# The transfers of an attention loop on SyncE put in the order of the source, and a weight chunk moved within a pair of heads

## The chip, the cores and the metric

The kernel runs on one core of one Trainium2 chip. The metric is the device time of one execution in microseconds (us). Before the change three runs took 875.57, 877.01 and 880.34, median 877.01.

A core has TensorE (PE, with its weight loads shown apart as PEld), VectorE (DVE), ScalarE (ACT), GpSimd (POOL) and SyncE (SP). SP computes nothing here; it issues transfers (DMAs). ACT issues some of its own, between its computations.

## The reference

Attention of 4 batches x 8 heads over 768 positions with heads of 64, in which a query sees only the keys whose 6-bit hash is its own, and then a feed-forward block with w_in (512 x 2048) and w_out (2048 x 512):

```python
q_bits = (np.einsum('bhsd,dk->bhsk', q, proj) > 0).astype(np.int64)
k_bits = (np.einsum('bhsd,dk->bhsk', k, proj) > 0).astype(np.int64)
...
mask = q_bucket[:, :, :, None] == k_bucket[:, :, None, :]
scores = scale * np.matmul(q, k.transpose(0, 1, 3, 2))
scores = np.where(mask, scores, -1000000000.0)
...
attn = attn / (np.sum(attn, axis=-1, keepdims=True) + 1e-09)
return np.matmul(attn, v).astype(np.float32)
...
h = x @ w_in
g = h * (1.0 / (1.0 + np.exp(-1.702 * h)))
return (g @ w_out).astype(np.float32)
```

The weights reach the core as 64-bit floats and are converted there.

## The kernel before

The attention works on 16 pairs of heads, n = 0 to 15; `attention` (L289) runs them in a software pipeline, and the loop over n = 1 to 15 (L625) holds in one turn work of several pairs. A pair has two halves of its queries, c = 0 and 1, and six tiles of 128 keys. Its scores come in groups (c, first key tile) of two key tiles each: (0,0), (0,2), then the values of the pair before (L524, `values`), then (0,4), (1,0), the values of this pair's half 0, then (1,2), (1,4). From pair 3 on (`BY_PARTS`) `scores_of_four` (L477) makes a group by three passes of 32-row matmuls at L491: over the hash features (`feat`), over `own` (q and k of the pair, transposed) and over `other` (the same rows with the 32-row halves of each head exchanged; the profile shows it as `s_in`, whose room it uses, and so it does for `own` of every third pair). All six groups take their PSUM places in turn from four. Each tile of scores goes through an exponential on ACT (L463). `unload` (L532, L535 and L536) takes finished values from PSUM to `xT` on ACT, which frees that place for a group of scores.

What a turn n of the loop prepares for later pairs:

- The hash of pair n+1: `featured(n + 1)` thresholds it on DVE (L446), and eight transfers of 12 KB carry it to `feats` (L454, `feat<-f`). `spread(n + 1)` copies these rows again by two transfers (L459, `feat<-feat`), which read what the eight wrote, and calls `exchange(n + 1)`, four transfers of 192 KB from `own` to `other` (L424, `s_in<-own` or `s_in<-s_in`).
- `fetch(n + 3, "k")` and `fetch(n + 3, "q")` load the raw k and q by four transfers each (L353), once `turn(n + 2)` (a DVE transpose, L417) and `measure(n + 2)` (an ACT pass over the same tile that bounds its size, L431) have read the tile's last contents. `fetch_v(n + 1)` loads v by two transfers (L365).
- A chunk of w_in, 512 KB, is loaded and converted. `begin(n)` (L576) starts it with a transfer on ACT (L165); its next steps are DVE operations (L181, L185, L189, L196, L200, L203) and one of ACT (L193), called by `step` at fixed places of the turn. There is one tile `raw` for it, so that a chunk's transfer follows the last step (L203) of the chunk before. In the turn of before, `begin(n)` stands behind the exponentials of (0,0) and (0,2).

The order on PE, DVE, ACT and POOL is the order of the source (`ORDERED`, L18). The order on SP is not: a scheduler places SP's transfers by its own estimate of when each could start. A queue runs strictly in its order; a transfer that waits holds up all behind it on that engine, and on ACT the computations too. Transfers of SP and ACT take eight completion semaphores in turn, in the order in which the scheduler placed them, and one takes a semaphore over only when the transfer that had it eight places earlier has landed.

As built, SP's row of 24 transfers in a turn from pair 6 on is: 8 features, 2 spreadings, 4 k, 2 v, 2 exchanges, 4 q, 2 exchanges, where the exchanges are those of pair n+2, one turn ahead of where the source has them. In turns 4 and 5 some exchanges stand among the features and spreadings, in turns 2 and 3 spreading and exchanges come behind k and v.

After the attention comes the feed-forward (`feed_forward`, L816), 539 us of the span.

Of the kernel before, what the change touches and what calls it, by code (L numbers as in the profile page):

```python
# [19 lines left out]
P = 128  # L20
# [18 lines left out]
def kernel(  # L39
# [17 lines left out]
    nc = tc.nc  # L57

    loader = [nc.sync]
    B, H, S, D = q.shape  # L60
# [7 lines left out]
    HS = HT * P  # L68
# [41 lines left out]
    for i, x in enumerate("kq"):  # L110
# [7 lines left out]
        for c in range(2):  # L118
            r0 = D * i + 32 * c
# [41 lines left out]
    def convert(cv, dst, src, queue=None, psum=None):  # L161


        raw = cv.tile([P, CW, 2], U32, tag="raw", name="raw")
        (queue or loader[0]).dma_start(out=raw, in_=src)  # L165
# [11 lines left out]
        yield  # L177


        if psum is None:  # L180
            nc.vector.scalar_tensor_tensor(part, hi, 3, masks[0x3FFFFFFF], op0=Alu.logical_shift_left, op1=Alu.bitwise_and)  # L181
# [107 lines left out]
    def attention(ff):  # L289
# [4 lines left out]
        with actx:  # L294
# [39 lines left out]
                nc.gpsimd.memset(*x)  # L334

            raws, vts, xts = {}, {}, {}

            def behind(x):

# [2 lines left out]
            def fetch(n, name):  # L342

                b, hp = pairs[n]
                x = raws[n, name] = ld.tile([P, S // 32, 32], F32, tag=name, name=name)
                if (n, name) == (2, "q"):
                    behind(x[:, 0, 0:1])
                src = {"k": k, "q": q}[name]
                for j in range(2):
                    rows = src[b, 2 * hp + j].rearrange("(s p) (a i) -> a p s i", p=32, i=32)  # L350
                    for a in range(D // 32):
                        r0 = D * j + 32 * a
                        loader[0].dma_start(out=x[r0 : r0 + 32], in_=rows[a])  # L353

            def fetch_v(n):
                b, hp = pairs[n]
                x = ld.tile([P, T, 2, D], F32, tag="v", name="v", bufs=2)
                if n == 0:
                    x = x.rearrange("p t j d -> p (t j d)").rearrange("p (j t d) -> p t j d", j=2, d=D)
                vts[n] = x  # L360
                if n == 1:
                    behind(x[:, 0, :, 0])
                for j in range(2):
                    order = "(t p) d -> p t d" if n else "(p t) d -> p t d"
                    loader[0].dma_start(out=x[:, :, j, :], in_=v[b, 2 * hp + j].rearrange(order, p=P))  # L365

            def first_pair():

# [50 lines left out]
            def exchange(n):  # L419

                for j in range(2):
                    for i in range(2):
                        r0, r1 = D * j + 32 * i, D * j + 32 * (1 - i)
                        loader[0].dma_start(out=other[n % 3][r0 : r0 + 32], in_=own[n % 3][r1 : r1 + 32])  # L424

            def measure(n, name):

# [16 lines left out]
            def featured(n):  # L444
                f = wk.tile([P, HS], BF16, tag="f", name="f", bufs=2)
                nc.vector.tensor_scalar(f, dots.pop(n), above[:, 0:1], weight[:, 0:1], op0=Alu.is_gt, op1=Alu.mult)  # L446
                yield
                for c in range(2):
                    for i, x in enumerate("kq"):

                        queue = nc.scalar if (n, x, c) == (1, "q", 0) else nc.sync
                        for j in range(2):
                            r0 = D * i + 32 * c + 16 * j
                            queue.dma_start(out=feats[n % 2][x][D * j : D * j + 16, c * HS : (c + 1) * HS], in_=f[r0 : r0 + 16, :])  # L454

            def spread(n):

                for j in range(2):
                    loader[0].dma_start(out=both[n % 2][D * j + 32 : D * j + 48], in_=both[n % 2][D * j : D * j + 16])  # L459
                exchange(n)  # L460

            def weigh(n, c, kt, ps):
# [14 lines left out]
            def scores_of_four(n, groups):  # L477

                for c, k0 in groups:
                    if n < BY_PARTS:  # L480
                        scores(n, c, (k0, k0 + 1))
                        continue
                    cols = slice(c * HS, (c + 1) * HS)
                    ps = [in_turn() for _ in range(2)]
                    f, x, y = feats[n % 2], own[n % 3], other[n % 3]
                    for at, (a, m) in enumerate(((f["k"], f["q"]), (x[:, 0], x[:, 1]), (y[:, 0], y[:, 1]))):
                        for i in range(2):
                            keys = slice((k0 + i) * P, (k0 + i + 1) * P)
                            for j in range(2):
                                r0 = D * j + 32 * i  # L490
                                nc.tensor.matmul(ps[i][:, j, 0:HS], a[r0 : r0 + 32, keys], m[r0 : r0 + 32, cols],  # L491
                                                 start=at == 0, stop=at == 2)
                    for i in range(2):
                        weigh(n, c, k0 + i, ps[i])
# [926 lines left out]
    def whole(steps):  # L1421
        for _ in steps:
            pass
# [49 lines left out]
```

## Time and profile before

| | |
|---|---|
| median of three runs | 877.01 us (875.57 to 880.34) |
| the profiled execution | 875.73 us, its span 873.9 us |
| PE busy | 851.7 us (97%) |
| DVE busy | 692.5 us (79%) |
| ACT busy | 335.9 us (38%) |
| POOL busy | 367.8 us (42%) |
| transfers issued by SP (queue q1) | 111.42 MB, 48.0% of 16 DMA engines' span |
| transfers issued by ACT (queue q10) | 31.62 MB, 10.8% |
| attention | up to 334.6 us |

How to read it: a row of a timeline is start, length (us), engine, line, operation, tile written <- tiles read, number of instructions, and in brackets the idle time before it with what ended it. "SPq" and "ACTq" are the issuing of a transfer, not its run. A row of the waits is engine, line <- what was waited for, then us in total, times, longest. What ended a wait is inferred from semaphores: a wait in front of a transfer that ACT issues is shown at the next computation of ACT.

### The profile page before, as it was taken

How to read it: one execution, taken by the hardware profiler on the slowest of the kernel's cores; microseconds unless marked ns; L12 is line 12 of the kernel's file. 1: busy time of each engine (PE TensorE's matmuls, PEld its weight loads, DVE VectorE, ACT ScalarE, POOL GpSimd, SP SyncE). 2: the span in 40 equal slices, each digit the busy share in tenths (PEclk: the TensorE clock that was granted, in tenths of full speed). 3: DMA queues.
4: the chain of work that ended last, by engine and by line, in shares of the span. 5: the costliest groups of instructions: out<-in, count | busy, mean ns of one | idle time of the engine just before them, and what ended most of it. 6: DMA issues, size and time to landing. Idle time of an engine off the chain costs nothing.

```text
span 873.9 us, 14972 instructions
## 1 busy us (share of the span) xinstructions
PE 851.7 (97%) x5631; PEld 524.7 (60%) x5631; DVE 692.5 (79%) x1069; ACT 335.9 (38%) x549; POOL 367.8 (42%) x321
## 2 busy tenths in 40 slices
PE   9999999999899999999999999999999999999996
PEld 4444444434344444465666666644888888888885
DVE  4478889888868997588788878766997977897786
ACT  5665656655566654344444444343100000000000
POOL 4333333433333437899773357678755100000000
PEclk9999999999999999999999999999999999999999
DMA  5768687777677401535455555568755575477534
GB/s 107 98 111 161 125 147 139 138 132 126 125 144 131 111 26 51 165 122 216 193 204 206 216 193 216 205 227 281 255 188 192 176 223 210 163 228 222 195 126 98
DMA packets 165197, 144.04 MB, mean 165 GB/s; under 512 B 124384, under 2 KB 139872, under 8 KB 159872
## 3 DMA queue, kind: packets, MB, share of 16 engines
q1 hardware_dynamic: 154704, 111.42, 48.0%
q10 hardware_dynamic: 10416, 31.62, 10.8%
q8 instruction: 45, 0.74, 0.4%
q14 instruction: 32, 0.26, 0.1%
HBM read 79.69 MB, written 50.33 MB: 149 GB/s over the span
## 4 chain that ended last, share of the span: by engine, by line
PE 67%; DVE 9%; DMA 8%; POOL 6%; SPq 4%; issue 3%; ACT 2%; ACTq 0%; DVEq 0%; POOLq 0%
PE product L1196 29%; PE product L869 16%; PE s L524 7%; PE small L937 5%; PE s L491 5%; DVE acc L515 3%; PE product L937 2%; PE s L474 2%; DMA feat<-f 2%; SPq L353 2%; DMA raw<-in_moe_w_in_dram 2%; SPq L454 1%; DMA q<-in_q_dram 1%; ACT e L463 1%; DMA k<-in_k_dram 1%
## 5 line engine op out<-in xcount | busy, mean ns | idle before, releaser
L463 ACT ACTIVATE e<-s 128x768 f32<-128x768 f32 x192 | 144.0, 812 | 51.1 <-PE s L491 41.9
L524 PE MATMUL s<-e,v 128*32 128x385 f32 x1536 | 131.9, 490 | 0.0
L502 POOL TENSOR_TENSOR t_x<-e 128x768 f32<-128x768 f32 x32 | 59.2, 1850 | 153.9 <-ACT e L463 139.3
L869 PE MATMUL product<-xT,w_in_sb 128*128 128x512 f32 x216 | 100.0, 593 | 0.1
L524 PEld LDWEIGHTS s<-e,v 128*32 128x32 f32 x1536 | 46.3, 109 | 81.1 <-issue 64.4
L869 PE MATMUL product<-t_x,s_in 128*128 128x512 f32 x192 | 89.5, 593 | 0.8 <-ACT u L991 0.8
L491 PE MATMUL s<-s_in 32*128 32x384 f32 x816 | 85.6, 488 | 1.6 <-DMA s_in<-own 0.8
L502 POOL TENSOR_TENSOR t_x<-t_x,e 128x768 f32<-128x768 f32 x32 | 56.2, 1756 | 51.6 <-ACT e L463 50.3
L515 DVE TENSOR_TENSOR acc<-acc,e 128x768 f32<-128x768 f32 x63 | 73.6, 1169 | 2.3
L1232 ACT COPY u<-product 128x256 f32<-128x256 f32 x20 | 7.4, 372 | 158.1 <-PE product L1196 124.9
L869 PEld LDWEIGHTS product<-xT,w_in_sb 128*128 128x128 f32 x216 | 40.9, 190 | 35.8 <-issue 32.5
L491 PEld LDWEIGHTS s<-s_in 32*128 32x128 f32 x816 | 43.1, 186 | 23.0 <-DMA s_in<-own 2.5
L869 PEld LDWEIGHTS product<-t_x,s_in 128*128 128x128 f32 x192 | 36.4, 190 | 30.8 <-issue 27.3
L491 PE MATMUL s<-own 32*128 32x384 f32 x432 | 46.6, 487 | 0.0
L491 PE MATMUL s<-feat 32*128 32x384 bf16 x312 | 32.2, 327 | 10.8 <-ACT xT L536 10.0
L885 DVE TENSOR_TENSOR u<-product,u 128x256 f32<-128x256 f32 (+1 forms) x60 | 28.4, 485 | 15.6 <-PE product L937 12.8
L491 PEld LDWEIGHTS <-feat 32*128 32x128 bf16 x312 | 10.4, 91 | 49.1 <-issue 37.0
L1196 PE MATMUL product<-raw_g,xT 128*128 128x256 f32 x152 | 35.1, 379 | 0.0
L225 POOL TENSOR_TENSOR u<-v,u 128x1024 f32<-128x1024 f32 (+1 forms) x11 | 23.8, 2167 | 21.5 <-ACT v L882 14.1
L226 POOL TENSOR_TENSOR v<-c,v 128x1024 f32<-128x1024 f32 (+1 forms) x15 | 32.4, 2157 | 1.0
L885 DVE TENSOR_TENSOR v<-product,v 128x512 f32<-128x512 f32 x24 | 16.5, 688 | 19.8 <-PE product L869 19.8
L512 DVE SCALAR_TENSOR_TENSOR acc<-t_x,e 128x768 f32<-128x768 f32 x31 | 29.3, 946 | 3.2 <-ACT e L463 2.5
(298 smaller groups left out, 1809.5 us busy)
## 6 DMA issues: line engine op xcount, KB each, us to landing
raw_g<-g_dram SPq DMA_DIRECT2D x20, 1024.0 KB, 5.1
s_in<-g_dram SPq DMA_DIRECT2D x20, 1024.0 KB, 5.1
g_dram<-c ACTq DMA_DIRECT2D x18, 512.0 KB, 2.9
raw<-in_moe_w_out_dram ACTq DMA_DIRECT2D x16, 512.0 KB, 3.7
raw<-in_moe_w_in_dram ACTq DMA_DIRECT2D x15, 512.0 KB, 3.8
s_in<-own SPq DMA_DIRECT2D x36, 192.0 KB, 4.4
v<-in_v_dram SPq DMA_DIRECT2D x32, 192.0 KB, 3.8
k<-in_k_dram SPq DMA_DIRECT2D x60, 96.0 KB, 3.1
```

The lines of the kernel that those rows point to most:

```text
L225: return [lambda: eng.tensor_tensor(t1, b12, b11, op=Alu.subtract), lambda: eng.tensor_tensor(b12, b22, b12, op=Alu.subtract), lambda: eng ...
L226: lambda: eng.tensor_tensor(b12, b22, b12, op=Alu.subtract),
L463: nc.scalar.activation(es[c][:, kt, :, 0:HS], ps[:, :, 0:HS], Act.Exp, scale=1.0 / D**0.5)
L491: nc.tensor.matmul(ps[i][:, j, 0:HS], a[r0 : r0 + 32, keys], m[r0 : r0 + 32, cols], start=at == 0, stop=at == 2)
L502: nc.gpsimd.tensor_tensor(low_sum, low_sum if i else e[:, 0], e[:, i + 1], op=Alu.add)
L512: nc.vector.scalar_tensor_tensor(acc, terms[0], T * TINY, terms[1], op0=Alu.add, op1=Alu.add)
L515: nc.vector.tensor_tensor(acc, acc, terms[i + 1], op=Alu.add)
L524: nc.tensor.matmul(av[D * j + d : D * j + d + 32, :], vt[:, t, j, d : d + 32], es[c][:, t, j, :], start=(t == 0), stop=(t == T - 1))
L869: nc.tensor.matmul(ps, wq[LEFT[i]][:, kc, :], xq[RIGHT[i]][:, kc, :], start=(start and kc == 0), stop=(kc == K2 - 1), skip_group_check=not ...
L885: nc.vector.tensor_tensor(dst, x, y, op=Alu.add)
L937: nc.tensor.matmul(x, wq[LEFT[i]], xq[RIGHT[i]], start=start, stop=True, skip_group_check=True)
L1196: nc.tensor.matmul(ps, wq[LEFT[i]][:, c, :], gq[RIGHT[i]][:, c, :], start=(onto is None and c == 0), stop=(c == F4 - 1), skip_group_check= ...
```

## The change

The transfers that SP issues in the attention from turn 2 on are held in the order of the source (`tc.keep_in_program_order`), by a helper `load` that takes the place of `loader[0].dma_start` in `fetch`, `fetch_v`, `exchange`, `featured` and `spread`. `spread(n + 1)` moves up in the turn, from behind `fetch_v(n + 1)` to ahead of `fetch(n + 3, "k")`. `begin(n)` moves from behind both first groups of exponentials to between them, and two dependencies without a semaphore (`behind_issue`) place the chunk behind the first feature transfer and the second feature transfer behind the chunk, in the scheduler's order alone. Nothing is added to or taken from what is computed or moved.

```diff
+            turns_kept = [False]
+            def load(out, in_):
+                dma = nc.sync.dma_start(out=out, in_=in_)
+                if turns_kept[0]:
+                    tc.keep_in_program_order(dma)
+                return dma
+            def behind_issue(dma, other):
+                tc.add_manual_dep(dma.ins, other.ins.name,
+                                  mybir.DependencyInfo(mybir.DependencyClass.NoSync, mybir.DependencyReason.DATA), reason="row")
...
             def begin(n):
                 if 0 <= n - 2 < len(in_chunks) - LATE:
                     conv[n] = convert(cv, *in_chunks[n - 2], nc.scalar)
-                    step(n)
+                    return next(conv[n])
...
+                    turns_kept[0] = True
+                    scores_of_four(n, ((0, 0),))
                     if n < last:
+                        first = next(features)
+                        chunk = begin(n)
+                        if chunk is not None:
+                            behind_issue(chunk, first)
+                            behind_issue(next(features), chunk)
                         whole(features)
-                scores_of_four(n, ((0, 0), (0, 2)))
+                    else:
+                        begin(n)
+                    scores_of_four(n, ((0, 2),))
+                else:
+                    scores_of_four(n, ((0, 0), (0, 2)))
                 if n == 2:
                     measure(3, "q")
                     fetch(4, "q")
-                begin(n)
...
                     if more:
                         measure(n + 2, "k")
+                    if n < last and n + 1 >= BY_PARTS:
+                        spread(n + 1)
                     if n + 3 <= last:
                         fetch(n + 3, "k")
...
                 if n < last:
                     fetch_v(n + 1)
-                    if n + 1 >= BY_PARTS:
-                        spread(n + 1)
```

As built, PE, DVE and POOL have the same instructions in the same order as before. On ACT the chunk's transfer stands behind the second exponential of a turn in place of the fourth. SP's row is now, in every turn from 3 on: 8 features of pair n+1, 2 spreadings and 4 exchanges of pair n+1, 4 k, 2 v, 4 q; the chunk takes its semaphore between the first and the second feature.

More of the change, by code (lines that the diff above doesn't have):

```diff
@@ L164, in convert @@
         raw = cv.tile([P, CW, 2], U32, tag="raw", name="raw")
-        (queue or loader[0]).dma_start(out=raw, in_=src)
+        dma = (queue or loader[0]).dma_start(out=raw, in_=src)
         def of(x):
@@ L176, in convert @@
             size = psum.tile([P, CW], F32, tag="size", name="size")
-        yield
+        yield dma
         if psum is None:
@@ L352, in fetch @@
                         r0 = D * j + 32 * a
-                        loader[0].dma_start(out=x[r0 : r0 + 32], in_=rows[a])
+                        load(x[r0 : r0 + 32], rows[a])
             def fetch_v(n):
@@ L364, in fetch_v @@
                     order = "(t p) d -> p t d" if n else "(p t) d -> p t d"
-                    loader[0].dma_start(out=x[:, :, j, :], in_=v[b, 2 * hp + j].rearrange(order, p=P))
+                    load(x[:, :, j, :], v[b, 2 * hp + j].rearrange(order, p=P))
             def first_pair():
@@ L423, in exchange @@
                         r0, r1 = D * j + 32 * i, D * j + 32 * (1 - i)
-                        loader[0].dma_start(out=other[n % 3][r0 : r0 + 32], in_=own[n % 3][r1 : r1 + 32])
+                        load(other[n % 3][r0 : r0 + 32], own[n % 3][r1 : r1 + 32])
             def measure(n, name):
@@ L449, in featured @@
                     for i, x in enumerate("kq"):
-                        queue = nc.scalar if (n, x, c) == (1, "q", 0) else nc.sync
                         for j in range(2):
                             r0 = D * i + 32 * c + 16 * j
-                            queue.dma_start(out=feats[n % 2][x][D * j : D * j + 16, c * HS : (c + 1) * HS], in_=f[r0 : r0 + 16, :])
+                            to, of = feats[n % 2][x][D * j : D * j + 16, c * HS : (c + 1) * HS], f[r0 : r0 + 16, :]
+                            if (n, x, c) == (1, "q", 0):
+                                nc.scalar.dma_start(out=to, in_=of)
+                            else:
+                                yield load(to, of)
             def spread(n):
                 for j in range(2):
-                    loader[0].dma_start(out=both[n % 2][D * j + 32 : D * j + 48], in_=both[n % 2][D * j : D * j + 16])
+                    load(both[n % 2][D * j + 32 : D * j + 48], both[n % 2][D * j : D * j + 16])
                 exchange(n)
@@ L635, in attention @@
                         step(n - 1)
+                    turns_kept[0] = True
+                    scores_of_four(n, ((0, 0),))
                     if n < last:
-                        whole(features)
-                scores_of_four(n, ((0, 0), (0, 2)))
+                        first = next(features)
[3 more added lines that the diff above has]
+                            behind_issue(next(features), chunk)
+                        whole(features)
+                    else:
+                        begin(n)
+                    scores_of_four(n, ((0, 2),))
+                else:
+                    scores_of_four(n, ((0, 0), (0, 2)))
                 if n == 2:
```

## The prediction

> **What bounds the kernel now.** I read the busy shares first, then the attention stage in windows, then the waits, then the timeline of one pair.
>
> ```profile
> span 873.9 us, 14972 instructions
> ```
> ```profile
> 66.78:88.50 21.72, 20.89 (x237) 9.09 (x240) 18.28 (x25) 12.80 (x22) 6.51 (x5) 1.00 0.84 159
> 88.50:272.20 183.70, 173.69 (x2092) 76.84 (x2096) 154.75 (x207) 113.43 (x190) 66.40 (x36) 0.99 0.73 134
> 253.68:272.20 18.52, 18.52 (x237) 8.26 (x240) 16.50 (x23) 12.61 (x22) 6.96 (x4) 1.00 0.72 136
> 272.20:310.13 37.93, 36.88 (x458) 16.40 (x459) 35.22 (x45) 22.98 (x39) 13.84 (x9) 1.00 0.48 103
> 334.60:873.90 539.30, 531.84 (x2011) 381.58 (x2011) 424.63 (x699) 131.82 (x213) 245.21 (x199) 1.00 0.56 193
> ```
>
> The columns are the stretch, its length, the busy time of PE, PEld, DVE, ACT and POOL, the granted clock, the DMA share and GB/s. I cut at the ends of the matmuls of L546, one per pair. Pairs 4 to 12 are the second row, 183.70 / 9 = 20.41 us each. Pair 12 (third row) has no idle time of PE and takes 18.52. So PE alone would need 18.5 a pair; the nine pairs have 9 x 1.89 = 17.0 us over that, and pair 3 (first row) has 3.2. This 20.2 us and the 1.05 that PE is idle in pairs 13 and 14 (fourth row, 37.93 - 36.88) are all that the change can win. The last row, the feed-forward, holds nothing that the diff touches.
>
> ```profile
> PE s L491 <- ACT xT L536: 10.0, 9, 2.3
> PE s L491 <- DMA s_in<-own: 0.8, 1, 0.8
> PE s L491 <- DMA s_in<-s_in: 0.8, 1, 0.8
> ```
> ```profile
> ACT xT L431 <- DMA feat<-f: 32.2, 10, 4.8
> DVE w_in_sb L181 <- DMA raw<-in_moe_w_in_dram: 20.7, 10, 3.8
> ```
>
> PE waits for the unloading of a PSUM tile by ACT (L536), ACT waits for a transfer of features. The timeline of ACT and PE in pair 8 (start, us, what) tells why:
>
> ```profile
> 177.43 0.33 ACTq L165 DMA_DIRECT2D raw<-in_moe_w_in_dram  x1
> 177.88 0.84 ACT L431 ACTIVATE xT<-k 128x768 f32<-128x768 f32 x1 [4.17 <-DMA feat<-f]
> 178.90 0.58 ACT L536 ACTIVATE xT<-s,vs 128x384 f32<-128x384 f32 x1
> ```
> ```profile
> 177.51 0.33 PE L491 MATMUL s<-feat 32*128 32x384 bf16 x2
> 179.53 0.34 PE L491 MATMUL s<-feat 32*128 32x384 bf16 x2 [1.69 <-ACT xT L536]
> ```
>
> ACT does not wait in L431. It waits in front of L165, whose transfer of the chunk takes its turn on a semaphore that a feature transfer of the same pair holds. Behind it stand the measuring (L431) and the unloading (L536), for which PE waits 1.69 us. What makes the features late is SyncE's row:
>
> ```profile
> 160.96 1.19 SPq L459 DMA_DIRECT2D feat<-feat  x2
> 167.09 4.16 SPq L353 DMA_DIRECT2D q<-in_q_dram  x4
> 171.29 2.40 SPq L424 DMA_DIRECT2D s_in<-own  x2
> 173.79 4.96 SPq L454 DMA_DIRECT2D feat<-f  x8
> 181.53 1.19 SPq L459 DMA_DIRECT2D feat<-feat  x2
> 182.82 2.32 SPq L353 DMA_DIRECT2D k<-in_k_dram  x4
> 185.19 1.11 SPq L365 DMA_DIRECT2D v<-in_v_dram  x2
> 186.51 1.15 SPq L424 DMA_DIRECT2D s_in<-own  x2
> 187.77 3.55 SPq L353 DMA_DIRECT2D q<-in_q_dram  x4
> 191.37 1.20 SPq L424 DMA_DIRECT2D s_in<-own  x2
> 192.67 1.74 SPq L454 DMA_DIRECT2D feat<-f  x1
> ```
>
> Apart from the 2.78 us from 178.75 to 181.53, in which it waits until the eight features have landed, SyncE issues without a break. From one spreading (L459) to the next are 181.53 - 160.96 = 20.57 us, which is PE's 20.41 per pair. So the row of transfers, not PE, sets the pace; the chunk's semaphore is only where PE meets it.
>
> **The change, part by part.** *The chunk moves up* between the second and third exponential of a pair, second in the turn. The transfer whose semaphore it takes over is then the last of the k loads of the row before, landed long since in the steady pattern of before. In pair 12 the exponentials and the values matmuls behind them stand so:
>
> ```profile
> 255.37 2.94 ACT L463 ACTIVATE e<-s 128x768 f32<-128x768 f32 x4 [1.55 <-PE s L491]
> ```
> ```profile
> 256.63 4.09 PE L524 MATMUL s<-e,v 128*32 128x385 f32 x48
> ```
>
> The second exponential ends 3.2 us into the pair (255.37 + 1.47 - 253.68); the chunk of pair 8 was issued 8.3 us into it. So the nine ACT waits of PE (10.0) go, and the chunk is there when DVE reaches L181 (20.7 us of waits that cost little: DVE has 2.0 us of slack in pair 12). ACT pays the 0.33 us of issuing ahead of its third exponential; PE is in the 4.09 us of values matmuls then, which hide it. Without that cover it would be 0.33 x 14 pairs = 4.6.
>
> *The row keeps its 24 transfers.* Nothing is removed from SyncE: eight features, two spreadings, four exchanges, four k, two v, four q. Only the order differs: spreading and exchanges come ahead of k and v, and no exchange stands between q and the features. The first gain is in pair 3:
>
> ```profile
> 64.08 2.64 SPq L424 DMA_DIRECT2D s_in<-own  x4
> 66.84 3.47 SPq L353 DMA_DIRECT2D q<-in_q_dram  x4
> 70.40 6.86 SPq L454 DMA_DIRECT2D feat<-f  x8
> ```
> ```profile
> 69.77 1.45 PE L491 MATMUL s<-s_in 32*128 32x384 f32 x5 [0.83 <-DMA s_in<-own]
> ```
>
> Its exchanges go out at 64.08 behind four k and two v (2.32 + 1.11 in the row above). In the changed order they go out about 3.4 us earlier, so that the 3.2 us of pair 3 go, nearly all.
>
> *What the row then costs per pair.* The exchange of pair n+1 was issued a whole pair ahead (the first half at 186.51 in pair 8, as soon as its transposes were done, for pair 10). Now it stands behind the landing of the features of the same pair, and PE needs it some 0.9 us into the next. Counted from the first feature: eight issues 4.96, landing and wait 2.78, two spreadings 1.29 with the gap, four exchanges 2.64, and 4.4 from issue to landing of the last (less its own issue, 0.6):
>
> ```profile
> s_in<-own SPq DMA_DIRECT2D x36, 192.0 KB, 4.4
> ```
> ```profile
> DMA to landing us min/median/max: 1.7/2.6/5.5
> ```
>
> 4.96 + 2.78 + 1.29 + 2.64 + 3.8 = 15.5 us. PE needs it 18.5 + 0.9 = 19.4 after a pair's start, so features may start up to 3.9 us into a pair at no cost. But at 70.40 they start 3.6 us after pair 3 began (66.78), so the row has used up its lead at once, and from then on PE follows the row: a pair takes what the row takes. The row took 20.4. Of it I take off what the chunk no longer costs the last features: their landing (the last fence above, L454) is 1.7 at the least and 2.6 in the median. The bounds are a gain of 0.9 and a loss of about 1 (the chunk now lies in the drain of the q loads, and the seventh feature's turn hangs on the last of these); that the exchange is no longer between q and features saves 1.2 to 2.4 of issue there (171.29 and 191.37) and costs as much ahead of k. I take 0.7, near the landing row: 19.7 a pair. Whether a 512 KB chunk among the q loads slows them, no row shows.
>
> A rule of the Trainium skill speaks against even this. DMA: Bandwidth & Descriptors, section "Issuing engines are not separate DMA queues", says that transfers started by different engines run on the same 16 DMA engines and interleave. By it the chunk takes the same engine time wherever ACT issues it and the row stays at 20.4. That is a rival below; the 1.7 against 2.6 is why I hold it less likely.
>
> The sum, against the profiled execution's own span: pair 3 gives 3.2. Pair 4 then runs at 18.5 (its exchange lands in time), 1.9 under the mean. Pairs 5 to 12 give 8 x 0.7 = 5.6. Until the row is in step, pair 5 waits about 1.2 more. Pair 13 loses its wait for ACT and gets one of about 1.2 for the exchange, nothing. Together 3.2 + 1.9 + 5.6 - 1.2 = 9.5; I say 9. The profiled execution took 875.73, 1.3 under the median of 877.01; from the median 877 - 9 = 868.
>
> One loss of before lies inside the 20.41:
>
> ```profile
> 242.50:245.95 3.45, 3.45 (x28) 1.25 (x24) 2.31 (x4) 2.29 (x5) 0.00 (x0) 0.51 0.21 48
> ```
>
> Right after PE's longest wait (2.3) the granted clock was 0.51 for 3.45 us, which cost 3.45 x 0.49 = 1.7. With waits of 1.2 I expect none; where the row sets the pace it is hidden in the row, where PE does it is won.
>
> TensorE: Matmul & The Clock Gate, "Part 1: The HAM clock gate", puts the fall of the clock behind an idle window of about 3.4 us; here 2.3 us of idleness were enough, so the page's figure would promise more safety than this trace does.
>
> **The rivals.**
>
> *PE sets the pace* (chance 0.20). If the row shortens to 18.5, all of 20.2 + 1.05 less about 3 of small waits goes: 18 to 19, 858. For it: single steps add up to less than the row (4.96 + 1.7 + 1.29 + 2.64 + 2.32 + 1.11 + 3.55 = 17.6 with the shortest landing). Against it: q took 3.55 and 4.16 us for four issues where k took 2.32, so issues stall when much is on its way, and all of k, v and q now stand in one block.
>
> *The row stays at 20.4* (chance 0.24), the chunk only moved within it. Then pair 3, pair 4 and the start-up remain: 3.2 + 1.9 - 1.2, about 4 at best, 2 with a clock fall: 873 to 876. That the change does not do what it says in time is this case: the ACT waits vanish and a wait of the same size for the exchange takes their place.
>
> *The exchange is later still, slower* (chance 0.13).
>
> ```profile
> 213.68 6.27 SPq L454 DMA_DIRECT2D feat<-f  x8
> ```
>  Place: the matmuls of L491 that read s_in, at each pair's start. If the features land 1 us later, because their turn hangs on q loads that share engines with the chunk, the row becomes 21.4 (it took 213.68 - 192.67 = 21.0 once, with 6.27 for the features). Pairs 5 to 13 then lose 9 x 1.0, less the 4 above: 5 slower, 882, and with it more falls of the clock. It decides from a row of about 20.9 on.
>
> **How the numbers follow.** My forecast, a row of 19.7 with 866 to 871, has 0.43. Faster by over 0.5% (about what the measurement of this kernel tells from none; 4.4 us) are 0.20, most of the 0.43, and a little of the second rival: 0.66. Same takes the rest of these: 0.22. Slower: 0.12. The likeliest case's own range, with the bounds of 0.9 and of nothing for the row, is 865 to 873; the range for 8 in 10 reaches to PE's pace below (859) and to the row's unchanged length above with the run-to-run spread (878).
>
> **What would show it.** Right: no wait of L491 for ACT xT L536, no ACT wait at L431 for features, no wait of L181 for the chunk, the chunk issued 3 to 5 us into a pair; pair 3 near 18.5; from pair 5 on about 1.2 us of waiting of L491 for s_in; spreadings 19.7 apart. Wrong: pairs of 18.5 throughout (the row had room), or spreadings over 20.5 apart (the order costs the row), or ACT still waiting at its chunk.

## The result and the profile after

The changed kernel takes 870.71 us (median of 13 runs, 869.41 to 873.40) against 877.01 us for the kernel before on the same chip (13 runs). The ratio is 0.994, 95% interval 0.9925 to 0.9956: 0.6% faster, 6.3 us of the 9 that were forecast.

In the listing after, all of SyncE's transfers of the attention have one line, L340; the scores are L506 (before: L491), the unloading L551 (L536), the measuring L443 (L431). First the windows of the profile after, cut at the same places as before; the columns are the stretch, its length, the busy time of PE, PEld, DVE, ACT and POOL, the granted clock, the DMA share and GB/s:

```profile
42.87:68.17 25.30, 24.26 (x220) 10.74 (x224) 19.73 (x25) 16.39 (x28) 8.26 (x5) 1.00 0.53 105
68.17:87.06 18.89, 18.85 (x236) 8.43 (x240) 17.04 (x24) 12.88 (x22) 7.55 (x5) 1.00 0.75 134
87.06:106.86 19.80, 19.68 (x236) 8.92 (x240) 18.04 (x23) 12.89 (x22) 6.89 (x5) 1.00 0.74 119
106.86:264.46 157.60, 156.28 (x1861) 70.27 (x1864) 135.44 (x185) 102.18 (x169) 56.29 (x33) 1.00 0.78 141
264.46:305.44 40.98, 39.55 (x458) 17.49 (x459) 38.33 (x46) 23.43 (x39) 13.77 (x8) 1.00 0.62 126
284.13:305.44 21.31, 19.96 (x226) 8.63 (x227) 19.94 (x24) 10.52 (x18) 7.15 (x5) 1.00 0.63 141
329.10:868.70 539.60, 531.90 (x2013) 381.64 (x2011) 424.79 (x699) 131.75 (x213) 245.25 (x199) 1.00 0.57 193
```

These are pair 2, pair 3, pair 4, pairs 5 to 12, pairs 13 and 14, pair 14 by itself, and the feed-forward. For the first of them the row of the profile before has not been shown yet:

```profile
42.70:66.78 24.08, 23.91 (x219) 10.92 (x218) 18.96 (x24) 16.46 (x28) 8.45 (x5) 1.00 0.65 116
```

| stretch | before | after | gained | forecast |
|---|---|---|---|---|
| pair 2 | 24.08 | 25.30 | -1.2 | 0 |
| pair 3 | 21.72 | 18.89 | 2.8 | 3.2 |
| pairs 4 to 12 | 183.70 | 19.80 + 157.60 = 177.40 | 6.3 | 1.9 + 5.6 - 1.2 = 6.3 |
| pairs 13 and 14 | 37.93 | 40.98 | -3.0 | 0 |
| sum | | | 4.9 | 9.5 |

The attention ends at 329.10 us instead of 334.60, 5.5 earlier (the 0.6 beyond the table lie behind pair 14 and ahead of pair 2), and the feed-forward takes what it took (539.60 against 539.30). So the forecast lost its 4 us in pair 2 and in pairs 13 and 14, not in the middle. The waits after (who waits, for whom: us, times, longest):

```profile
PEld s L506 <- DMA s_in<-s_in: 6.2, 7, 1.8
PEld s L506 <- DMA s_in<-own: 4.8, 7, 0.9
PE s L506 <- DMA s_in<-s_in: 1.8, 2, 1.2
```

No wait of L506 for ACT xT L551 is left, where there were nine with 10.0 us. In their place TensorE, mostly its weight load, waits for the exchange (s_in), 14 times. And SyncE's row from pair 8 into pair 9, between the first and the last of the ten spreadings that give its mean (start, us, what):

```profile
81.94 0.51 SPq L340 DMA_DIRECT2D feat<-feat  x1
...
171.97 6.55 SPq L340 DMA_DIRECT2D feat<-f  x8
179.14 1.19 SPq L340 DMA_DIRECT2D feat<-feat  x2
180.37 2.49 SPq L340 DMA_DIRECT2D s_in<-own  x4
182.97 2.81 SPq L340 DMA_DIRECT2D k<-in_k_dram  x4
185.88 1.19 SPq L340 DMA_DIRECT2D v<-in_v_dram  x2
187.18 4.58 SPq L340 DMA_DIRECT2D q<-in_q_dram  x4
191.86 5.42 SPq L340 DMA_DIRECT2D feat<-f  x8
199.58 1.51 SPq L340 DMA_DIRECT2D feat<-feat  x2
...
259.23 0.51 SPq L340 DMA_DIRECT2D feat<-feat  x1
```

(259.23 - 81.94) / 9 = 19.70 us from spreading to spreading, as forecast. This is a mean: the single rows take 18.8 to 20.9 us, and pairs 7 and 8 ran at TensorE's own 18.52. SyncE stands still in front of the spreading until features have landed, 0.62 us at the first of the two shown (178.52 to 179.14) and 2.30 us at the second (197.28 to 199.58). The second is the longest of the ten; the other nine are 0.6 to 1.0 us, where the rows of the kernel before have 2.2 to 2.9 from pair 6 on. Why the row takes 19.70 is another matter: the experiments are about that.

### The profile page after: what moved, and what is told of

The parts are those of the page before. It is cut to its first block, busy times and chain, and to the rows that moved or that the text cites. A ratio compares the mean times of both kernels' runs of the same rounds, so it can differ in the third digit from the quotient of the medians.

```text
span 868.7 us, 14987 instructions
## 1 busy us (share of the span) xinstructions
PE 854.7 (98%) x5631; PEld 527.2 (61%) x5631; DVE 692.8 (80%) x1069; ACT 337.9 (39%) x549; POOL 363.9 (42%) x321
## 4 chain that ended last, share of the span: by engine, by line
PE 75%; DMA 8%; POOL 6%; DVE 3%; SPq 3%; ACT 2%; issue 2%; ACTq 0%; DVEq 0%; POOLq 0%
PE product L1221 29%; PE product L894 16%; PE s L539 10%; PE s L506 10%; PE small L962 5%; SPq L340 3%; DMA q<-in_q_dram 3%; PE product L962 2%; DMA s_in<-own 2%; PE s L489 1%; ACT e L478 1%; DMA s_in<-s_in 1%; DMA raw<-in_moe_w_in_dram 1%; DMA feat<-f 1%; DMA k<-in_k_dram 1%
## 5 line engine op out<-in xcount | busy, mean ns | idle before, releaser
L517 POOL TENSOR_TENSOR t_x<-e 128x768 f32<-128x768 f32 x32 | 54.1, 1690 | 146.5 <-ACT e L478 143.6
L506 PE MATMUL s<-s_in 32*128 32x384 f32 x816 | 95.4, 484 | 2.9 <-DMA s_in<-s_in 1.8
L506 PEld LDWEIGHTS s<-s_in 32*128 32x128 f32 x816 | 47.4, 185 | 31.9 <-DMA s_in<-s_in 6.2
L506 PE MATMUL s<-own 32*128 32x384 f32 x432 | 48.8, 482 | 0.0
L225 POOL TENSOR_TENSOR u<-v,u 128x1024 f32<-128x1024 f32 (+1 forms) x11 | 23.8, 2166 | 21.8 <-ACT v L907 14.1
L458 DVE TENSOR_SCALAR f<-s,above,weight 128x384 bf16<-128x384 f32 x15 | 10.1, 674 | 28.0 <-PE s L561 18.5
L910 DVE TENSOR_TENSOR c<-small,c 128x256 f32<-128x256 f32 (+1 forms) x54 | 24.2, 462 | 9.2 <-PE small L962 9.0
```

Of the source, the lines that this page charges most:

```text
L517: nc.gpsimd.tensor_tensor(low_sum, low_sum if i else e[:, 0], e[:, i + 1], op=Alu.add)
L910: nc.vector.tensor_tensor(dst, x, y, op=Alu.add)
```

## The experiments

| kernel | us | ratio to the kernel before, 95% |
|---|---|---|
| only the chunk moved | 875.95 | 1.0000 (0.9977 to 1.0022) |
| only the order kept | 878.75 | 1.0031 (1.0012 to 1.0050) |
| before, two more transfers a pair | 879.19 | 1.0033 (1.0014 to 1.0052) |
| after, two more transfers a pair | 866.38 | 0.9892 (0.9859 to 0.9925) |
| after, two more behind q | 873.60 | 0.9965 (0.9942 to 0.9988) |
| after, chunk of a sixteenth | 861.62 | 0.9824 (0.9798 to 0.9851) |
| before, chunk of a sixteenth | 860.87 | 0.9817 (0.9793 to 0.9842) |
| spreading behind k and v | 861.12 | 0.9822 (0.9798 to 0.9847) |
| the same, exchange a pair ahead | 861.55 | 0.9829 (0.9806 to 0.9852) |
| chunk's turn, scheduler's order | 882.78 | 1.0066 (1.0043 to 1.0089) |
| spreading early for pair 3 alone | 862.36 | 0.9837 (0.9796 to 0.9878) |
| the same, chunk of turn 2 late | 857.03 | 0.9777 (0.9742 to 0.9813) |

Each ratio is to the kernel before as it ran beside that kernel (medians of 875.99, 876.54 and 877.10 us).

### Each half of the change alone

The kernel before with the chunk moved:

```diff
-                scores_of_four(n, ((0, 0), (0, 2)))
+                scores_of_four(n, ((0, 0),))
+                begin(n)
+                scores_of_four(n, ((0, 2),))
...
-                begin(n)
                 add_high(n - 1, 1, (0, 1))
```

> The kernel before with one edit: the chunk of W_in is begun between a pair's first two and its second two exponentials; SyncE's transfers stay where the scheduler puts them. Theory (SyncE's row of 24 transfers sets the pace, ACT's wait is only the place where TensorE meets it): the row stays at about 20.4 us per pair, TensorE waits for the features or for the exchange instead of for ACT, and the time falls by the one-time slack between the two meeting points at most: 871 to 876. Rival (ACT's wait in front of the chunk was itself the cost): with it gone the pairs run at TensorE's own 18.5 us, 858 to 862.

The changed kernel with the chunk back at its old place, and its order kept:

```diff
-                    scores_of_four(n, ((0, 0),))
                     if n < last:
-                        first = next(features)
-                        chunk = begin(n)
-                        if chunk is not None:
-                            behind_issue(chunk, first)
-                            behind_issue(next(features), chunk)
                         whole(features)
-                    else:
-                        begin(n)
-                    scores_of_four(n, ((0, 2),))
+                    scores_of_four(n, ((0, 0), (0, 2)))
...
+                begin(n)
                 add_high(n - 1, 1, (0, 1))
```

> The changed kernel with its other half undone: SyncE's transfers stay in the order of the source, but the chunk of W_in is begun behind all features and all four exponentials, as before. Theory: the exchange comes as late as in the changed kernel and ACT waits again in front of the chunk for transfers of the row, so both meeting points are there: 20 to 20.5 us per pair, 875 to 881. Rival (the order of the transfers alone brings the gain, the chunk's place nothing): 870 to 871.5, pairs of 19.7 us.

Measured: 875.95 and 878.75. In the whole time neither half gains anything, and the order alone costs 0.3%. In pairs 4 to 12 the chunk alone does gain, 179.20 us instead of 183.70 (19.91 each, where the theory had about 20.4):

```profile
93.99:273.19 179.20, 171.92 (x2092) 77.82 (x2096) 145.78 (x207) 112.53 (x190) 66.25 (x36) 1.00 0.71 137
```

It loses as much ahead of them: pair 4 begins 5.5 us later, and pair 3 takes 24.07 us, at a granted clock of 0.93. This run does not separate the theory from its rival either, since ACT still waits in front of its chunk. ACT and SyncE in pair 8 of the kernel with only the chunk moved:

```profile
179.18 0.35 ACTq L165 DMA_DIRECT2D raw<-in_moe_w_in_dram  x1
179.63 1.51 ACT L463 ACTIVATE e<-s 128x768 f32<-128x768 f32 x2 [3.80 <-DVE own L417]
```
```profile
176.61 4.96 SPq L454 DMA_DIRECT2D feat<-f  x8
```

ACT was idle for 3.80 us ahead of the third exponential, and the chunk stands in that gap (the name in the bracket is not what ended it). The chunk's semaphore is that of the second feature of the same row: the features go out from 176.61 on, and the chunk has to wait for that one's landing. So moving the instruction moved ACT's wait. Less of it is passed on: TensorE waits 3.2 us for ACT's unloading in pairs 4 to 12, and 9.0 in the kernel before. With only the order kept, the old wait is there in full (pairs 5 to 12):

```profile
PE s L506 <- ACT xT L551: 9.3, 7, 2.9
```

For the whole gain both halves are needed. That the order lets the chunk's turn be fixed, and that the turn takes the wait away, is how I read these traces; no run changes the turn alone.

### Two more transfers in the row

```diff
                     fetch_v(n + 1)
+                    if n + 1 >= BY_PARTS:
+                        for j in range(2):
+                            load(spare_rows[:, j], both[n % 2][0:16, j, 0 : S // 4])
```

> The kernel before with two more small transfers per pair on SyncE (16 partitions of 96 elements each, into a tile that nothing reads), behind the v loads, from pair 2 to 13. No engine waits for them. Theory (the row's length, issue by issue, is the pace): each adds its issue of about 0.6 us to the row, so pairs 4 to 12 go from 20.4 to about 21.6 us and the time to 885 to 892 (12 pairs by 1.2 us is 14, less what the first pairs hide). Rival (SyncE has slack and ACT's wait or TensorE sets the pace): within 2 us of the kernel before, 875 to 879.

> The changed kernel with the same two more small transfers per pair on SyncE behind the v loads. Theory: the row of 19.7 us grows by about 1.2 us and the time to 880 to 886. Rival (the pace is TensorE's, or that of the features' wait, which would take the two issues in): within 2 us of the changed kernel, 869 to 873.

Measured: 879.19 in the kernel before, 3 us slower and not 8 to 15; 866.38 in the changed one, 4 us *faster* than without them and outside both ranges (its interval, 0.9859 to 0.9925, just touches the changed kernel's, 0.9925 to 0.9956). Pairs 4 to 12 of the kernel before, and pairs 5 to 12 of the changed one, each with the two more transfers:

```profile
92.33:273.03 180.70, 171.78 (x2093) 76.37 (x2096) 154.13 (x207) 113.28 (x190) 66.24 (x36) 0.99 0.71 137
```
```profile
107.05:262.37 155.32, 153.74 (x1860) 69.84 (x1864) 147.44 (x184) 101.37 (x169) 59.96 (x32) 1.00 0.76 141
```

180.70 / 9 = 20.08 and 155.32 / 8 = 19.41 us per pair, against 20.41 and 19.70 without them. In the kernel before, whose profiled execution is its fastest (876.54), the loss stands ahead of these pairs: pair 4 begins 3.8 us later, and pair 3 takes 24.67 us at a granted clock of 0.86.

In the kernel before, the scheduler left the two transfers ahead of the next loads only in the first four turns. In the eight from 140 us on they stand between the features and the spreading, where SyncE waited for the landing anyway:

```profile
181.73 1.22 SPq L675 DMA_DIRECT2D spare_rows<-feat  x2
183.06 2.52 SPq L460 DMA_DIRECT2D feat<-feat  x2
```

There they fill a pause that the prediction had seen, so this run says little of the rest of that row. In the changed kernel, whose order is kept, they do stand behind the v loads: two issues of some 0.6 us added, and the row did not grow. My theory that the row's length is the sum of its issues falls with this run. What gave way is seen at the q loads behind the two: they land in 4.2 us at the median instead of 5.6, and four of them take 2.2 to 3.6 us to issue instead of 2.6 to 4.7.

The same two transfers, placed between the q loads and the features:

```diff
+                        for j in range(2):
+                            load(spare_rows[:, j], both[n % 2][0:16, j, 0 : S // 4])
                         first = next(features)
```

> The changed kernel with the two more small transfers per pair standing between the q loads and the features instead of between the v loads and the q loads, where they made it 4 us faster. Theory (they helped because the q loads went out further from the k and v loads, and more of the chunk came behind them): here they only delay the features by 1.2 us, 872 to 880. Rival (they helped by shifting which transfer's semaphore the later ones take over): 865 to 868 again.

Measured: 873.60, against 866.38 at the other place (the intervals, 0.9942 to 0.9988 and 0.9859 to 0.9925, lie apart) and 870.71 without them. So it is their place that helps. The time is in the theory's range, but its reason is not borne out: here too the q loads land early, in 4.1 us at the median. Nor is the rival excluded. The first feature and the chunk take over the semaphores of the two v loads in both runs, but the four q loads' go to the second to fifth feature here and to the fourth to seventh there. A clear difference is ACT's wait in front of its chunk, 21.8 us in seven waits here and 5.8 in two there:

```profile
ACT e L479 <- DMA v<-in_v_dram: 21.8, 7, 3.5
```

Why the two help at one place stays open.

### The chunk's bytes

```diff
-        dma = (queue or loader[0]).dma_start(out=raw, in_=src)
+        dma = (queue or loader[0]).dma_start(out=raw[:, 0:cols or CW], in_=src[:, 0:cols or CW])
...
-                    conv[n] = convert(cv, *in_chunks[n - 2], nc.scalar)
+                    conv[n] = convert(cv, *in_chunks[n - 2], nc.scalar, cols=32)
```

> The changed kernel with chunks of a sixteenth: from pair 3 on ACT's transfer for W_in moves 32 KB instead of 512 KB (the rest of the chunk is left out, and the squares of the conversion are scaled by zero so that the old data stay finite); instructions and turns are the same. It is read at the attention's end and in the pairs. New theory (the two more transfers cost nothing, so SyncE's row is elastic: its length is made by waits for landings, and the features land behind the q loads and the chunk): without the chunk's bytes the rows shorten and pairs 5 to 12 go from 19.7 to 18.6 to 19.0 us, pair 14 loses its 3 us, time 859 to 864. Old theory (issue by issue): 19.7 stays, 869 to 872.

> The kernel before with the same chunks of a sixteenth (the rest of the chunk left out). New theory (bytes of the chunk delay the landings): ACT still has to wait for a feature of the row in front of its chunk, since that wait hangs on the turn and not on the bytes, but the features and the next row's loads land earlier: pairs 4 to 12 19.3 to 20.0 instead of 20.4, 868 to 874. Old theory: 20.4 stays, 875 to 878.

Both kernels leave out fifteen sixteenths of each chunk from pair 3 on. Measured: 861.62 and 860.87, the second below both of its ranges. The windows of pairs 5 to 12 and of pair 14 in the changed kernel with small chunks, then of pairs 4 to 12 in the kernel before with small chunks:

```profile
105.90:259.10 153.20, 152.64 (x1860) 69.01 (x1864) 133.27 (x184) 101.68 (x169) 56.84 (x32) 1.00 0.69 118
277.62:296.25 18.63, 18.63 (x226) 8.49 (x227) 18.25 (x23) 10.40 (x18) 6.46 (x5) 1.00 0.50 100
```
```profile
91.40:260.51 169.11, 168.11 (x2092) 74.99 (x2096) 140.34 (x207) 113.44 (x190) 63.76 (x36) 1.00 0.73 120
```

19.15 us per pair instead of 19.70, and 18.79 instead of 20.41: in the kernel before, the bytes of nine chunks are 14.6 of the 17.0 us that its pairs had over TensorE's own pace. The instructions, the order and ACT's turn in front of the chunk were left as they were. What the bytes do can be read from the transfers' times from issue to landing (KB each, median us), in the same pairs of the changed kernel:

```profile
raw<-in_moe_w_in_dram ACTq DMA_DIRECT2D x8, 512.0 KB, 5.4
q<-in_q_dram SPq DMA_DIRECT2D x32, 96.0 KB, 5.6
feat<-f SPq DMA_DIRECT2D x64, 12.0 KB, 3.4
```

and with small chunks:

```profile
q<-in_q_dram SPq DMA_DIRECT2D x32, 96.0 KB, 4.2
feat<-f SPq DMA_DIRECT2D x64, 12.0 KB, 1.8
```

The chunk lies among the q loads and in front of the features: q lands 1.4 us later, a feature of 12 KB 1.6 us later, and the chunk itself takes 5.4 us. The row has three waits that stretch with it: the turns of the sixth and seventh feature hang on the last two q loads, the spreading on the features, the exchange on the spreading.

This also bears on pair 14. In turn 13 the features' issue took 9.45 us, and the exchange landed 1.2 us after TensorE wanted it. SyncE and TensorE of the changed kernel there:

```profile
271.20 9.45 SPq L340 DMA_DIRECT2D feat<-f  x8
```
```profile
287.30 1.51 PE L506 MATMUL s<-s_in 32*128 32x384 f32 x5 [1.21 <-DMA s_in<-s_in]
```

With small chunks pair 14 takes 18.63 instead of 21.31. With the whole chunk it takes 18.47 beside the two idle transfers and 17.87 with the late spreading (below), so this price belongs to the chunk in this order of the row, not to the chunk alone.

One thing the small chunk does not separate: in the kernel before, DVE's waiting for the chunk (20.7 us there) goes too. Features land there in 2.1 us at the median instead of 2.8, and the q loads no earlier (5.1 and 4.8). ACT's waits for features in front of its chunk shrink from 25.8 to 13.7 us, and TensorE's waits for ACT's unloading from 9.0 to 1.0. How much of the 14.6 us came through the landing of the features and how much through DVE stays open.

### Where the spreading stands

```diff
-                    if n < last and n + 1 >= BY_PARTS:
-                        spread(n + 1)
                     if n + 3 <= last:
                         fetch(n + 3, "k")
...
                     fetch_v(n + 1)
+                    if n + 1 >= BY_PARTS:
+                        spread(n + 1)
```

> The changed kernel with one move: spreading and exchange stand behind the k and v loads again, so that SyncE issues these while the features land. Theory (waits for landings make the row): some 1 to 2 us of waiting in front of the spreading go, the row becomes 18.7 to 19.2, the exchange comes 3 us later within it: 863 to 868. Rival (the exchange's landing is already where TensorE meets the row, and 3.8 us of issues ahead of it make that worse in each pair): 872 to 880.

Measured: 861.12, below the expected range. Pair 3, then pairs 4 to 12 with the late spreading:

```profile
68.77:92.82 24.05, 22.35 (x237) 10.53 (x240) 18.38 (x24) 12.99 (x22) 7.92 (x5) 0.93 0.87 158
92.82:259.48 166.66, 166.66 (x2093) 74.36 (x2096) 139.95 (x207) 113.40 (x190) 65.19 (x36) 1.00 0.73 146
```

166.66 / 9 = 18.52: TensorE's own pace, with no idle time in nine pairs, and with the whole chunk of 512 KB. Its row in pair 7:

```profile
153.03 1.21 SPq L340 DMA_DIRECT2D feat<-f  x2
155.22 2.02 SPq L340 DMA_DIRECT2D k<-in_k_dram  x4
157.34 2.45 SPq L340 DMA_DIRECT2D v<-in_v_dram  x2
159.84 1.18 SPq L340 DMA_DIRECT2D feat<-feat  x2
...
163.66 2.86 SPq L340 DMA_DIRECT2D q<-in_q_dram  x4
167.67 6.15 SPq L340 DMA_DIRECT2D feat<-f  x8
```

The last feature is issued by 154.24. The k and v loads, the first of them after a wait of 0.98 us, go out until 159.79, and the spreading 0.05 us later, without a wait of its own. In the changed kernel SyncE stood still in front of it, with the k and v loads queued behind.

That pause was mostly 0.6 to 1.0 us, so it is not the whole gain. The q loads, no longer in one block with k and v, land in 3.8 us at the median instead of 5.6, and eight features take 4.9 to 6.2 us to issue instead of 5.4 to 7.8. The move also gives the chunk and the first features the semaphores of exchanges in place of k and v loads. How much each of these brings is not separated.

And here SyncE pauses 1.15 us in front of the first feature (166.52 to 167.67), where the changed kernel goes straight on (191.76 to 191.86): the row is done before the next features are made. DVE makes them from TensorE's sums, and waits for these eleven times (seven times, 18.5 us, in the changed kernel):

```profile
DVE f L458 <- PE s L561: 30.2, 11, 3.7
```

So the row has room and no longer sets the pace. No issue was taken away; what fell are waits at the head of the queue, and issues that had taken longer beside other transfers.

The same, with the exchange a pair ahead:

```diff
                     load(both[n % 2][D * j + 32 : D * j + 48], both[n % 2][D * j : D * j + 16])
-                exchange(n)
...
                     turn(n + 2, "q")
+                    exchange(n + 2)
...
                         turn(3, x)
+                    exchange(3)
```

> As the run before, and the exchange of pair n+2 is issued as soon as the transposes of its q are done, in the middle of pair n, instead of behind the spreading of pair n+1: in the row it keeps its place between spreading and q loads, but for a pair further on. Theory (the exchange lost its lead of a pair by the change, and TensorE's waits in the first block of scores are for it): these waits go, TensorE meets only the spreading, pairs of 18.5 to 18.9, 858 to 864. Rival (the row's length is the pace whatever stands in it): as the run before, within 1.5 us.

Measured: 861.55, with pairs of 18.52 from pair 6 on. Since the run before has TensorE's pace there already, this one tells nothing about the exchange's lead, except that it isn't needed. In the first pairs it shifts the time: pair 2 takes 28.95 us instead of 25.12, pair 3 19.39 instead of 24.05, pairs 4 and 5 together 1.5 more.

The run that was to test the chunk's turn by itself leaves the order to the scheduler, with the spreading late:

```diff
-                    turns_kept[0] = True
```

> The chunk between the exponentials and second in the turn of semaphores, right behind the first feature, as in the changed kernel, but SyncE's other transfers where the scheduler puts them (order of the source not kept, spreading behind k and v as before). It differs from the run with only the chunk moved by the turn alone. Theory (what the moved chunk needs is its turn: behind later features ACT waits for their landing and passes the wait on to TensorE): no wait of ACT in front of the chunk, rows with k and v inside the features' landing, 861 to 865. Rival (the order of SyncE's transfers is what counts, the chunk's turn little): 872 to 877.

Measured: 882.78, outside both. The edit did not do what it was meant to. SyncE's row in its pair 9:

```profile
196.49 4.33 SPq L340 DMA_DIRECT2D feat<-f  x7
203.87 0.51 SPq L340 DMA_DIRECT2D feat<-feat  x1
204.43 0.58 SPq L340 DMA_DIRECT2D feat<-f  x1
```

Only one feature was held behind the chunk; six others overtook it, so that the chunk took its turn from the first feature and had to wait for its landing. The held feature then stands behind a spreading that waits 3.0 us (200.82 to 203.87). It tells nothing about the turn alone, but it shows the price of a waiting transfer with others behind it.

### Putting the gains together

The late order runs at TensorE's pace from pair 4 on and loses 5 us in pair 3, where the changed kernel is good. Spreading early for pair 3 alone:

```diff
-                    if n < last and n + 1 >= BY_PARTS:
+                    if n + 1 == BY_PARTS:
                         spread(n + 1)
...
+                    if n + 1 > BY_PARTS:
+                        spread(n + 1)
```

> Spreading and exchange for pair 3 ahead of its k and v loads, as in the changed kernel, and from pair 4 on behind them, as in the run with the late spreading. Theory (the early exchange is worth 5 us in pair 3, where TensorE waits for s_in, and nothing later, where the late order runs at TensorE's 18.5): 855 to 858. Rival (pair 4's late row then loses what pair 3 won): 860 to 862.

and besides, the chunk of turn 2 alone behind the four exponentials:

```diff
-                        chunk = begin(n)
+                        chunk = begin(n) if n > 2 else None
...
                     measure(3, "q")
                     fetch(4, "q")
+                    begin(n)
```

> As the run before, with the chunk of turn 2 alone back behind the four exponentials, so that it does not fall among this turn's loads and features. Theory (pair 2 was 1.2 us longer because the chunk slowed the k loads and features of its turn): 1.0 to 1.4 us under the run before. Rival (ACT then waits in front of the chunk, and pair 3 pays for it): the same within 0.7 us or slower.

Measured: 862.36, then 857.03. Pair 4 of the first; pairs 2 and 4 of the second:

```profile
86.79:111.43 24.64, 21.98 (x237) 10.53 (x240) 16.49 (x23) 12.80 (x22) 7.17 (x5) 0.93 0.87 160
```
```profile
43.43:67.49 24.06, 23.91 (x221) 10.73 (x224) 19.14 (x24) 16.59 (x28) 8.47 (x5) 1.00 0.59 118
86.86:106.83 19.97, 19.89 (x237) 8.99 (x240) 16.50 (x23) 12.80 (x22) 6.48 (x4) 1.00 0.87 163
```

In the first the rival was right (862.36 against its 860 to 862): pair 3 takes 18.88, and the stall only moved to pair 4. In the second, pair 2 is back at 24.06, the 1.2 us that the change had cost there and that I had expected. But 4.7 us of pair 4's stall are gone as well, which I had not: SyncE's spreading for pair 4 goes out at 81.93 us instead of 84.57, and TensorE's two waits there (2.7 us) and the fall of its clock are gone. With the loads of turn 2 undisturbed the whole row starts earlier. This kernel takes 857.03 us, 2.2% less than before (0.9777, 0.9742 to 0.9813). Its interval lies clear of the changed kernel's and still overlaps that of the late spreading alone (0.9798 to 0.9847).

## Why the prediction was right or wrong

**The time and the sign were right**: 870.71 is in the range of 859 to 878, and in the forecast's own 865 to 873. Part of this is luck, as the next points show.

**"The nine ACT waits of PE (10.0) go"**: right, none is left. DVE still waits for the chunk at L181, 5.1 us in five turns where it was 20.7 in ten. The chunk does take over the semaphore of the last k load of the row before, but "landed long since" was wrong in part of the steady turns: k goes out later in the new order, and ACT waited for it three times, 1.41 us in pair 9, beside values matmuls and at no cost to TensorE:

```profile
189.34 1.51 ACT L478 ACTIVATE e<-s 128x768 f32<-128x768 f32 x2 [1.41 <-DMA k<-in_k_dram]
```

The run with only the chunk moved shows that the place in the program alone does not take ACT's wait away.

**Pair 3**: 2.8 of the 3.2.

**Pairs 4 to 12**: 6.3 forecast, 6.3 measured, with a row of 19.70. The split inside was off: pair 4 did not run at 18.5 but at 19.80. Pair 5 took 20.99, as an extra 1.2 would have it, but the pairs behind it spread from 18.52 to 20.75, so that it can't be told apart from that spread.

**"SyncE's row, not PE, sets the pace", because "SyncE issues without a break"**: the row does set the mean pace, but the reason failed. Most of the row is issuing (17.7 of 20.4 us from 179.14 to 199.58), yet two more issues per pair did not lengthen it in the changed kernel: issues stretch and shrink, and between them stand waits for landings. Both grow with the 512 KB of the chunk beside the q loads and features.

The 0.7 that I took off was what "the chunk no longer costs the last features". That term was larger: the pause in front of the spreading fell from 2.2 to 2.9 us in the rows from pair 6 on to 0.6 to 1.0 in nine rows of ten. Other terms, which I had bounded at a loss of about 1, took most of it back: in its new place the chunk falls on the q loads, which land in 5.6 us at the median instead of 4.8, and the eight features, whose later ones wait for them, take 5.4 to 7.8 us to issue instead of 5.0 to 6.4. That the difference came out at 0.7 is luck.

**The rule of the Trainium skill** that I held less likely (DMA: Bandwidth & Descriptors, "Issuing engines are not separate DMA queues") agrees with the runs: the bytes of a transfer issued by ACT delay SyncE's by 1.4 to 1.6 us at the median. Its consequence for the time, as I drew it, was too simple: the row did not stay at 20.4, since it matters which transfer is delayed and what waits for it.

**"Whether a 512 KB chunk among the q loads slows them, no row shows"** was named, and outside pairs 5 to 12 costed at nothing; this is the step that failed. The chunk of turn 2 among k loads and features cost 1.2 us in pair 2 (24.06 with it at the old place). The chunk of turn 13 among the q loads cost about 2.7 of pair 14 (18.63 with small ones). Together they are 3.9 of the 4.6 us that the sum has too much.

**The rivals**: "PE sets the pace, 858" was said to need a row of 18.5, and against it stood that all of k, v and q are in one block. With the spreading behind k and v, which also parts this block, the row takes 18.5, and the time is 861; with the first pairs mended, 857.

## What to carry to other kernels

On an engine that issues transfers in order, put other issues between a transfer and the one that needs its landing; a wait at the head of the queue holds up everything behind it. Before calling a queue full, add two idle transfers to it, and look where they were put: if the time doesn't grow, its length is not the sum of its issues. A row shown as an example should be set beside the others; the pause of 2.30 us here was the longest of ten. And a large transfer on another engine has a price that depends on what it falls among: shrink it once to read that price, and look at the first and last turns, where it falls among other things than in the middle.

## What was not expected of the hardware

*The clock fell after two short waits.* In pair 3 with the late spreading TensorE waited 0.82 us for the spreading and, 2 us on, 0.85 us for the exchange; then the granted clock was 0.50 for 3.4 us. TensorE's two waits, and the window behind them:

```profile
69.86 0.69 PE L506 MATMUL s<-feat 32*128 32x384 bf16 x2 [0.82 <-DMA feat<-feat]
...
72.71 1.97 PE L506 MATMUL s<-s_in 32*128 32x384 f32 x5 [0.85 <-DMA s_in<-own]
```
```profile
72.90:76.30 3.40, 3.40 (x24) 2.66 (x23) 3.29 (x9) 1.62 (x2) 0.06 (x1) 0.50 0.96 97
```

By an estimate (half of 3.40) that costs 1.7 us, as much as the two waits. The same clock of 0.93 over the pair stands in pair 4 of the run with the early spreading for pair 3. The Trainium skill (TensorE: Matmul & The Clock Gate, "Part 1: The HAM clock gate") speaks of an idle window of about 3.4 us; here two waits of together 1.7 us, as the trace counts them, were followed by the fall.

*Two transfers that nobody needs made a kernel 0.5% faster* (0.9892 against 0.994, with intervals that touch), by standing between the v and the q loads. That their place matters is shown; what on the queue they ease is not.
